# Wider token groups for the seven-product stages of an attention and gated-FFN kernel: three of 1024 tokens and two of 768 in place of six of 768

## The chip, the cores and the metric

The kernel runs on one core of a Trainium2 chip. The metric is the device time of one execution in microseconds. Below, PE is TensorE (PEld its weight loads), DVE is VectorE, ACT is ScalarE, POOL is GpSimd, and SP is SyncE, whose queue issues every DMA of this kernel.

## What is computed

Sliding-window attention over 8 batches of 576 tokens with 8 heads of 64, and behind it a gated feed-forward layer over all 4608 tokens (d_model 512, d_ff 1536), in float32:

```python
scores = scale * np.matmul(q, k.transpose(0, 1, 3, 2))
bias = slopes[:, None, None] * (-np.abs(rel).astype(np.float32))[None, :, :]
mask = (rel >= 0) & (rel < window)            # window = 128
scores = np.where(mask, scores + bias[None], -1000000000.0)
attn = np.exp(scores - np.max(scores, axis=-1, keepdims=True))
attn = attn / (np.sum(attn, axis=-1, keepdims=True) + 1e-09)
x = np.matmul(attn, v)                         # to (4608, 512)
gate = 1.0 / (1.0 + np.exp(-(x @ w_gate)))
val = x @ w_val
out = gate * val @ w_out
```

## The kernel before

Float32 products are made on PE from split operands: each factor becomes a high part and a low part (a cast, then a subtraction, in `parts`), and a product takes three matmuls: high by high, low by high, high by low.

The work has three stages.

1. **Attention** (up to about 305 us), in units of one batch and one pair of heads. PE makes scores (line 408), transposes (456) and values (493); DVE, ACT and POOL do the softmax. x goes to device memory (`xs`). In between, PE makes the **early stage** (`ffn`, matmuls on line 545): the first four of twelve 128-wide chunks of d_ff, for the first 3072 tokens, in blocks of 512 tokens, with plain products.
2. **The seven-product stage** (`ffn2`, line 679). Gate and value projections of one chunk are taken as a 2x2 product of blocks: two halves of d_model, two halves of a token group, in seven products instead of eight. x of a group is read (`later_xr`, one buffer, tag `xr`), combined and split into seven pairs `xc0` to `xc6` (tags `ar0` to `ar6`), each with one buffer. A chunk then runs the products in the order 0, 3, 4, 1, 5, 2, 6, six matmuls each, with DVE adding, ACT copying and taking tanh between them; the hidden rows (`later_hs`, two buffers, four in the last group) are stored to `hid`. Half a group is N2 = 384 tokens, so a matmul has 384 columns.
3. **The down stage** (`last`, line 797), also in seven products. Hidden rows of a group are read into twelve tiles (`rows`), combined and split into pairs `duo` (a ring of eight over tags `ar0` to `ar7`), and multiplied by prepared blocks of w_out (`wo`), 252 matmuls a group. Six groups follow each other.

Prepared weights of a chunk (`prepare2`: seven blocks, high and low, 14 KB a partition) lie in eight resident slots `w2s0` to `w2s7`; three are filled during attention, five behind it in memory that attention used. Chunks 4 to 7 and 0 to 3 are the first eight; groups 4 and 5 use all of them, since the early stage doesn't reach their tokens; then chunks 8 to 11 replace 0 to 3 in slots 4 to 7, and groups 5, 4, 0, 1, 2, 3 use those (0 to 3 with chunks 4 to 7 as well). In the same time w_out is prepared and kept in device memory (`stash_o`), and its six pairs (`wo`) are read into slots 0 to 5 at the end of the last group, each when PE has left the slot.

Nothing is scheduled by hand. Each operation is put into a graph with its engine, a cost and the keys that it reads and writes; `Graph.order` simulates the engines with these costs and always starts what can start first, and the program is written out in that order. So each engine, and SP's queue of DMAs, has a fixed order, and an instruction that waits holds up all behind it on its engine. A DMA also waits for the one eight places ahead in the queue (the eight `DMAHW` counters).

The resident slots and the end of the sequence, which the change rewrites, are these lines:

```python
NT2 = NT // (2 * N2)                  # six groups
first = list(zip(range(FC2), stay + First.fcs))
after = list(zip(range(FC2 - FC1, FC2), swap))
both = first[:FC2 - FC1]
```

Of the kernel before, what the change touches and what calls it, by code (L numbers as in the profile page):

```python
# [8 lines left out]
F32 = mybir.dt.float32  # L9
# [31 lines left out]
OUT0, OSTEP = 490.0, 38.0  # L41
# [11 lines left out]
NRAW = 2  # L53

# [109 lines left out]
def attention_gated_ffn(ctx: ExitStack, tc: tile.TileContext, qd, kd, vd, wg, wv, wo, out):  # L164
# [71 lines left out]
    for p in range(1, NPAIR):  # L236
# [24 lines left out]
    PIECE = 3  # L261
# [178 lines left out]
    def probabilities(u, i0):  # L440
# [4 lines left out]
        both = lambda: T(att, f"both{m % NBOTH}", [P, TRI, P], F32)  # L445
# [28 lines left out]
    def values(u):  # L474
# [46 lines left out]
    def ffn(t, w):  # L521
# [29 lines left out]
        for i0 in range(0, n, GRP):  # L551
# [6 lines left out]
            for i in grp:  # L558
# [18 lines left out]
    def combo(k, part_):  # L577
        return T(moe, f"xc{k}", [P, 4 * N2], F32R, tag=f"ar{k}").rearrange("p (h c t) -> p h c t", h=2, c=2)[:, part_]
# [47 lines left out]
    def ffn2(t, w, todo, F, ends=False):  # L626
        made = t in held
        held[:] = [t]
        t0 = t * 2 * N2
        xr = lambda: xrow()  # L630
        x = lambda h, k: (lambda: xr()[:, 2 * k:2 * k + 2, h * N2:(h + 1) * N2])
        xk = {(h, k): [("xr", k, (h, e)) for e in range(2)] for h in range(2) for k in range(2)}
        low = lambda: T(moe, "low", [P, 4, N2], F32, tag="h2")
# [33 lines left out]
        def chunk(i, fc):  # L667
# [7 lines left out]
            def product(k, b, start, wk):  # L675
                def six():
                    for c in range(2):
                        for j, (xp, wp) in enumerate(((0, 0), (0, 1), (1, 0))):
                            nc.tensor.matmul(mm[b][:, 0:N2], w.tile2(i, wp)[:, wk, c * P:(c + 1) * P], combo(k, xp)[:, c],  # L679
# [36 lines left out]
            move(lambda: hid[c, q, t][m].rearrange("p (h t) -> p h t", h=2), lambda: hs(e), [kp, kv], [("hid", fc, t, 0)], F, N2, True)  # L716
# [248 lines left out]
```

## Time and profile before

| | |
|---|---|
| time, median of 3 runs | 1009.13 us (1007.08 to 1009.23) |
| the profiled execution | 1008.67 us, of which the span from first to last instruction is 1007.0 us |
| granted TensorE clock, mean | 0.995 |
| matmuls | 576 early, 2352 seven-product, 1512 down |
| moved by DMA | 176.89 MB, mean 176 GB/s |
| the early stage's last matmul starts | 330.8 us |
| the down stage's first matmul starts | 740.3 us |

A row of the groups gives line, engine, operation, what it writes and reads, shape and count, then the busy time, the mean duration of one in ns, and the engine's idle time just before them with what ended it. A row of a timeline gives start, duration, engine and operation. A row of the chain of work that ended last gives start, duration and what ran.

### The profile page before, as it was taken

Reading aid. Unit: us, or ns where it says so; the run is one execution under the profiler, and the core shown is the slowest. Engines: PE = TensorE matmul, PEld = TensorE weight load, DVE = VectorE, ACT = ScalarE, POOL = GpSimd, SP = SyncE. Lnnn points to the kernel's source line nnn. Section 1 sums busy time; section 2 is a strip of 40 time slices with the busy share of each in tenths; the row PEclk is TensorE's granted clock in tenths of the full one; section 3 lists DMA queues with packets and bytes.
Section 4 is the critical chain, followed back from the end, with each engine's and each line's share of the span. In section 5 each row is a group of like instructions: output and inputs, shape, how many; then the busy total and the mean of one; then the engine's idle time right before and its main releaser. Section 6 shows DMA issues by size and latency. Waiting matters only on the chain.

```text
span 1007.0 us, 19232 instructions
## 1 busy us (share of the span) xinstructions
PE 985.4 (98%) x6790; PEld 920.5 (91%) x6790; DVE 781.0 (78%) x2039; ACT 540.4 (54%) x1428; POOL 121.9 (12%) x217
## 2 busy tenths in 40 slices
PE   8799899999999999999999999999999999999998
PEld 7577678787888999999999999999999999999998
DVE  7998889877758988945876858758489887869773
ACT  5999788877764545534543536335344443434341
POOL 1334444323330100000000000000000000000000
PEclk9899999999999999999999999999999999999999
DMA  7677777857524543311463443437785454453501
GB/s 271 218 268 242 260 235 243 284 179 240 177 99 159 188 142 128 108 63 48 162 230 136 162 159 130 162 150 268 301 322 195 113 187 125 150 153 101 183 19 63
DMA packets 84288, 176.89 MB, mean 176 GB/s; under 512 B 7648, under 2 KB 50016, under 8 KB 84192
## 3 DMA queue, kind: packets, MB, share of 16 engines
q1 hardware_dynamic: 84192, 175.67, 51.3%
q8 instruction: 53, 0.87, 0.4%
q14 instruction: 43, 0.35, 0.1%
HBM read 117.44 MB, written 58.20 MB: 174 GB/s over the span
## 4 chain that ended last, share of the span: by engine, by line
PE 89%; ACT 5%; DVE 5%; issue 1%; POOL 0%; ACTq 0%; POOLq 0%
PE mm L679 40%; PE mm L797 26%; PE mm L545 10%; PE mm L493 5%; PE mm L408 4%; PE mm L456 3%; ACT pb L431 2%; ACT both L185 1%; ACT pb L451 1%; PE mm L255 1%; DVE xc L194 0%; DVE early_hs L564 0%; DVE w2s L194 0%; DVE mm L420 0%; DVE first L194 0%
## 5 line engine op out<-in xcount | busy, mean ns | idle before, releaser
L679 PE MATMUL mm<-xc,w2s 128*128 128x384 f32 x2352 | 409.4, 334 | 1.2 <-ACT low L185 1.1
L679 PEld LDWEIGHTS mm<-xc,w2s 128*128 128x128 f32 x2352 | 407.4, 188 | 3.0 <-ACT low L185 2.2
L797 PE MATMUL mm<-duo,wo 128*128 128x384 f32 x1512 | 262.4, 334 | 0.0
L797 PEld LDWEIGHTS mm<-duo,wo 128*128 128x128 f32 x1512 | 262.1, 188 | 0.0
L545 PE MATMUL mm<-first,first 128*128 128x512 f32 x564 | 154.1, 409 | 1.6 <-DVE first L194 1.5
L467 POOL TENSOR_SCALAR_AFFINE_SELECT pt<-both 128x384 f32<-128x384 f32 x192 | 103.8, 564 | 188.5 <-ACT both L185 165.1
L545 PEld LDWEIGHTS mm<-first,first 128*128 128x128 f32 x564 | 101.0, 191 | 25.6 <-issue 4.7
L686 DVE TENSOR_TENSOR mm<-mm,low 128x384 f32<-128x384 f32 x112 | 63.0, 562 | 76.9 <-PE mm L679 73.3
L690 ACT ACTIVATE sg<-mm 128x384 f32<-128x384 f32 x112 | 54.8, 491 | 116.7 <-PE mm L679 68.3
L185 ACT COPY low<-mm 128x384 f32<-128x384 f32 x111 | 53.2, 479 | 77.5 <-PE mm L679 68.4
L431 ACT ACTIVATE pb<-pb,st 128x128 f32<-128x128 f32 x216 | 84.8, 401 | 7.2 <-DVE st L428 7.0
L493 PEld LDWEIGHTS mm<-pt,vr 128*64 128x64 f32 x832 | 61.4, 137 | 11.7 <-issue 8.2
L194 DVE TENSOR_TENSOR duo<-rows,duo 128x768 fp32r<-128x768 f32 x66 | 62.9, 956 | 9.8 <-ACT duo L185 7.9
L493 PE MATMUL mm<-pt,vr 128*64 128x256 f32 (+2 forms) x832 | 66.9, 306 | 0.0
L185 ACT COPY both<-mm 128x384 f32<-128x384 f32 x95 | 45.4, 478 | 33.7 <-PE mm L456 21.3
L185 ACT CAST duo<-rows 128x768 fp32r<-128x768 f32 x44 | 36.7, 835 | 48.7 <-PE mm L797 26.0
L420 DVE COPY_PREDICATED mm<-early_h,mm 128x256 f32<-128x256 int32 (+1 forms) x144 | 48.5, 392 | 10.5 <-PE mm L408 10.2
L428 DVE CUSTOM_DVE_ANT_0 pb<-mm,early_h 128x128 f32<-128x128 f32 x216 | 51.3, 282 | 0.0
L456 PE MATMUL mm<-ident,pb 128*128 128x128 f32 x216 | 38.3, 286 | 10.9 <-ACT both L185 8.9
L456 PEld LDWEIGHTS mm<-ident,pb 128*128 128x128 f32 x216 | 25.5, 142 | 22.7 <-ACT both L185 12.7
L408 PE MATMUL mm<-kr,qr 64*64 64x192 f32 (+1 forms) x792 | 44.8, 337 | 1.4 <-DVE mm L249 1.1
L431 ACT ACTIVATION_READ_ACCUMULATOR pb<-pb,st 128x1 f32 x216 | 42.7, 198 | 0.0
(122 smaller groups left out, 1104.9 us busy)
## 6 DMA issues: line engine op xcount, KB each, us to landing
hid<-later_hs SPq DMA_DIRECT2D x56, 384.0 KB, 2.3
rows<-hid SPq DMA_DIRECT2D x48, 384.0 KB, 3.9
kr<-in_k_dram SPq DMA_DIRECT2D x21, 576.0 KB, 5.6
wo<-stash_o SPq DMA_DIRECT2D x12, 896.0 KB, 8.1
vr<-in_v_dram SPq DMA_DIRECT2D x32, 288.0 KB, 3.1
xs<-xt SPq DMA_DIRECT2D x32, 288.0 KB, 3.0
stash_o<-wtmp SPq DMA_DIRECT2D x12, 768.0 KB, 3.4
rows_xr<-hid SPq DMA_DIRECT2D x24, 384.0 KB, 3.5
```

The costliest lines, as they stand in the source:

```text
L185: g.add("ACT", act_cost(n, psum), lambda: nc.scalar.copy(out(), src()), reads, writes, want, release=release, ways=[("DVE", dve_cost(n, ps ...
L194: g.add("DVE", dve_cost(n, psum, True), lambda: nc.vector.tensor_tensor(out(), a(), b(), op=ALU.subtract), reads, writes, want, port=not p ...
L408: nc.tensor.matmul(to, qraw(u)[rows, i // 2, h * D:(h + 1) * D], keys, start=True, stop=True)
L431: g.add("ACT", 0.39, lambda: nc.scalar.activation(pb()[:, e], pb()[:, e], AF.Exp, bias=st()[:, e:e + 1], scale=-1.0, accum_out=st()[:, 3 + ...
L456: nc.tensor.transpose(tp[:, e], pb()[:, e], ident)
L467: nc.gpsimd.affine_select(pt(u)[:, f0:f0 + 2 * n - 1:2, :], both(), [[0, n], step], cmp, 0.0, base=0, channel_multiplier=mult)
L493: nc.tensor.matmul(to()[e * D:(e + 1) * D, a - e * S - t0:b - e * S - t0], vraw(u)[:, c], seen, start=first, stop=last, skip_group_check=True)
L545: nc.tensor.matmul(mm[s][:, 0:wd], w.tile(kind, wi, i)[:, c * P:(c + 1) * P], xpart(x, c)[:, 0:wd], start=(k == 0 and c == 0), stop=(k == ...
L679: nc.tensor.matmul(mm[b][:, 0:N2], w.tile2(i, wp)[:, wk, c * P:(c + 1) * P], combo(k, xp)[:, c], start=(start and c == 0 and j == 0), stop ...
L686: g.add("DVE", dve_cost(N2, psum=True), lambda: nc.vector.tensor_tensor(o(), bk(b)(), a(), op=ALU.add), [("mm", b), *reads] if okeys else ...
L690: g.add("ACT", act_cost(N2, psum=True), lambda: nc.scalar.activation(sg[h](), bk(b)(), AF.Tanh, scale=0.5), [("mm", b)], [("sg", h)], F)
L797: nc.tensor.matmul(mm[b][:, 0:N2], wo2(2 * q + m, wp)[:, k, j * P:(j + 1) * P], duo(xp)[:, m], start=(k in (0, 3, 1) and q == 0 and m == 0 ...
```

## The change

The token groups become three of 1024 tokens (halves of 512 columns) and two of 768 (halves of 384). Tiles of the stages are sized for 512. To find room:

- seven weight slots stay resident instead of eight. Slots 0 to 2 hold chunks 4 to 6 as before, slots 3 to 6 first chunks 0 to 3 and then chunks 7 to 10. Chunks 4 and 11 share slot 0: both are written to device memory once (`stash`, two DMAs of 896 KB each), and each of the groups 0 to 2 begins with the one that lies in slot 0, fetches the other (`fetch`) and uses it after slots 1 and 2;
- the early stage's split operands take six tiles of four pieces instead of eight of three, so tag `ar6` is free during attention and holds the first of three buffers of k and q; the buffers `both` and one of `xt` move into parts of `xr` and `h2`;
- in the down stage the ring of `duo` has six places instead of eight, and the twelve row tiles lie in `xr` (4), slot 6 (3), `hs0`, `hs1`, `ar6` (2) and `h3` instead of `xr` (4) and slots 6 and 7 (8).

Groups 3 and 4 (768 tokens) come first with seven chunks each, then 4 and 3 with the other five, then groups 0, 1 and 2 with eight.

The diff, cut to its core:

```diff
-SPLIT = 4
+GROUPS = ((0, 512), (1024, 512), (2048, 512), (3072, 384), (3840, 384))
+NG = len(GROUPS)
+SPLIT = 3
...
-N2 = 384
...
+NSLOT2 = 7
...
-OUT0, OSTEP = 490.0, 38.0
+OUT0, OSTEP = 470.0, 36.0
...
+ROOM = {"h2": 4 * NB, "h3": 6 * 2 * P, "h4": 4 * NB, "xr": 2 * KC * NB, "ar6": 4 * NB}
...
-    PIECE = 3
+    PIECE = 4
...
-    slots = {"kr": keep("h2", TOK), "qr": keep("xr", (NBLK + 1) // 2, P)}
+    slots = {("kr", 2): keep("h2", TOK), ("qr", 2): keep("xr", (NBLK + 1) // 2, P),
+             ("kr", 0): keep("ar6", TOK), ("qr", 0): keep("ar6", (NBLK + 1) // 2, P)}
     kept = [keep("h2", TRI, P), keep("xr", TRI, P)]
+    spread2 = [keep("xr", TRI, P), keep("h2", TRI, P)]
+    xt0 = keep("xr", S)
...
-        both = lambda: T(att, f"both{m % NBOTH}", [P, TRI, P], F32)
+        both = lambda: spread2[m % NBOTH]
...
-        t0 = t * 2 * N2
+        t0, N2 = GROUPS[t]
...
-    RING = (7, 0, 3, 4, 1, 5, 2, 6)
+    def stash(i, fc):
+        for p in range(2):
+            move(lambda p=p: stash2[KEPT.index(fc)][p], lambda p=p: as32(w2.tile2(i, p).rearrange("p a f -> p (a f)")),
+                 [("w2", i, p, 0), ("w2", i, p, 2)], [("stash2", fc, p)], FIRST + 0.95, 896, True)
+
+    def fetch(i, fc):
+        for p in range(2):
+            move(lambda p=p: as32(w2.tile2(i, p).rearrange("p a f -> p (a f)")), lambda p=p: stash2[KEPT.index(fc)][p],
+                 [("stash2", fc, p)], [("w2", i, p, 0), ("w2", i, p, 2)], FIRST + 0.95, 896, True)
+
+    RING = (0, 3, 4, 1, 5, 2)
...
+    HOMES = ((4, "xr", "xr", KC), (7, "w2s6", "w2s6", 3), (8, "hs0", "hs0", 1), (9, "hs1", "hs1", 1), (11, "ar6", "ar6", 2), (12, "h3", "h3", 1))
...
-    first = list(zip(range(FC2), stay + First.fcs))
-    after = list(zip(range(FC2 - FC1, FC2), swap))
-    both = first[:FC2 - FC1]
-    for i, fc in first[:KEEP2]:
-        prepare2(w2, i, fc, 2.0e6 + i, P0 + PSTEP * i)
+    KEPT = (stay[0], swap[3])
+    for i in range(KEEP2):
+        prepare2(w2, i, stay[i], 2.0e6 + i, P0 + PSTEP * i)
+    stash(0, stay[0])
...
-    ffn2(late[-1], w2, first[FC2 - FC1:] + both, FIRST + 1)
-    for i, fc in after:
+    head = list(zip(range(KEEP2), stay))
+    body = list(zip(range(KEEP2, NSLOT2), first))
+    ffn2(SPLIT, w2, head + body, FIRST + 0.4)
+    ffn2(SPLIT + 1, w2, body + head, FIRST + 1)
+    body = list(zip(range(KEEP2, NSLOT2), stay[KEEP2:] + swap))
+    for i, fc in body + [(0, swap[3])]:
         prepare2(w2, i, fc, FIRST + 0.9)
+    stash(0, swap[3])
...
+    for t in (SPLIT + 1, SPLIT):
+        ffn2(t, w2, body + [(0, swap[3])], FIRST + 1)
+    here, gone = swap[3], stay[0]
     for t in range(SPLIT):
...
-        ffn2(t, w2, both + after if t < SPLIT - 1 else both + [after[z] for z in (2, 0, 1, 3)], FIRST + 1, t == SPLIT - 1)
+        ffn2(t, w2, [(0, here)], FIRST + 1, ends)
+        fetch(0, gone)
+        here, gone = gone, here
+        ffn2(t, w2, head[1:] + [(0, here)] + body, FIRST + 1, ends)
```

Since a planner writes the order, three places of it are shown. Names end in a tile number of the program; in brackets stands what a row waits for.

SP's queue in group 0, where the next group's x is asked for. Before:

```order
L190 DMA later_xr_3972<-xs2_100 128x4x384 [waits DMAHW3_49,DVE_49]
L190 DMA stash_o0_106<-wtmp1_5642 128x1536 [waits DMAHW4_49,DVE_49]
L190 DMA later_xr_3972<-xs1_99 128x4x384 [waits DMAHW5_49,DVE_49]
L190 DMA hid010_118<-later_hs0_4140 128x768 [waits DMAHW6_49,DVE_49]
L190 DMA hid110_136<-later_hs1_4202 128x768 [waits DMAHW7_49,DVE_49]
L190 DMA wraw0_206<-in_moe_w_out_dram 128x1024 [waits DMAHW0_49]
```

After (`w2s00` and `w2s01` are the two parts of slot 0, `stash20` is chunk 4 in device memory):

```order
L192 DMA later_xr_3961<-xs2_100 128x4x192 [waits DMAHW2_49,DVE_49]
L192 DMA later_xr_3961<-xs3_101 128x4x320 [waits DMAHW3_49]
L192 DMA later_xr_3961<-xs1_99 128x4x128 [waits DMAHW4_49,DVE_49]
L192 DMA later_xr_3961<-xs2_100 128x4x384 [waits DMAHW5_49]
L192 DMA stash_o1_107<-wg0_5352 128x256 [waits DMAHW6_49,Activation_49]
L192 DMA w2s00_1395<-stash20_142 128x1792 [waits DMAHW7_49,PE_49]
L192 DMA w2s01_1404<-stash20_142 128x1792 [waits DMAHW0_49]
L192 DMA stash_o1_107<-wg0_5352 128x256 [waits DMAHW1_49,Pool_49]
L192 DMA hid120_137<-later_hs0_4119 128x1024 [waits DMAHW2_49,DVE_49]
```

The two reads of slot 0 are new; they stand behind the x of the next group and a store that waits for ACT, and ahead of the stores of hidden rows.

SP's queue at the border to the down stage (`rows` are the row tiles of its first group, `rows_xr` at the end those of the next). Before:

```order
L190 DMA wo250_7461<-stash_o5_111 128x1792 [waits DMAHW2_49,PE_49]
L190 DMA wo251_7465<-stash_o5_111 128x1792 [waits DMAHW3_49]
L190 DMA hid123_145<-later_hs2_7264 128x768 [waits DMAHW4_49,DVE_49]
L190 DMA rows70_7541<-hid100_130 128x2x384 [waits DMAHW5_49,PE_49]
L190 DMA rows71_7543<-hid110_136 128x2x384 [waits DMAHW6_49]
L190 DMA rows_xr_7073<-hid001_113 128x2x384 [waits DMAHW7_49,DVE_49]
```

After:

```order
L192 DMA wo250_7005<-stash_o5_111 128x1792 [waits DMAHW2_49,PE_49]
L192 DMA wo251_7008<-stash_o5_111 128x1792 [waits DMAHW3_49]
L192 DMA hid122_139<-later_hs2_6751 128x1024 [waits DVE_49]
L192 DMA rows_ar6_7074<-hid020_122 128x2x512 [waits DMAHW5_49,PE_49]
L192 DMA rows_h3_7076<-hid110_132 128x2x512 [waits DMAHW6_49,DMAHW4_49]
L192 DMA rows_ar6_7074<-hid120_137 128x2x512 [waits DMAHW7_49]
L192 DMA rows_xr_6633<-hid001_113 128x2x512 [waits DVE_49]
```

Before, tiles in slot 7 stand behind the wait for PE's last product, and its tiles in slot 6 have been read earlier; now the two tiles in `ar6` wait for that product, and the one in `h3` stands between them.

DVE at the seam from attention to the seven-product stage, up to the split of `xc0` and `xc1`. Before:

```order
L194 TENSOR_TENSOR xc5_4070<-later_xr_3972,xc5_4070 128x768 [waits PE_49]
L308 TENSOR_SCALAR tt_1420<-tt_1420 128x512 [waits Activation_49]
L311 SCALAR_TENSOR_TENSOR wbits0_442<-wraw0_206,wbits0_442 128x512 [waits DMAHW5_49]
L564 SCALAR_TENSOR_TENSOR early_hs0_1028<-sg0_878,mm0_148 128x512 [waits DMAHW7_49,PE_49]
L311 SCALAR_TENSOR_TENSOR tt_1420<-wraw1_224,tt_1420 128x512 [waits DMAHW6_49,DVE_49]
L194 TENSOR_TENSOR xc6_4102<-later_xr_3972,xc6_4102 128x768 [waits Activation_49]
L311 SCALAR_TENSOR_TENSOR tt_1420<-wraw1_224,tt_1420 128x512 [waits DVE_49]
L564 SCALAR_TENSOR_TENSOR early_hs1_1205<-sg1_947,mm1_149 128x512 [waits DMAHW0_49,PE_49]
L194 TENSOR_TENSOR xc0_4117<-later_xr_3972,xc0_4117 128x768 [waits Activation_49]
L194 TENSOR_TENSOR xc1_4127<-later_xr_3972,xc1_4127 128x768 [waits Activation_49]
```

After:

```order
L196 TENSOR_TENSOR xc4_4080<-low_4034,xc4_4080 128x2x384 [waits Activation_49]
L313 TENSOR_SCALAR tt_1410<-tt_1410 128x512 [waits Activation_49]
L316 SCALAR_TENSOR_TENSOR wbits0_434<-wraw0_201,wbits0_434 128x512 [waits DMAHW1_49]
L572 SCALAR_TENSOR_TENSOR early_hs1_1195<-sg1_937,mm1_145 128x512 [waits DMAHW2_49,PE_49]
L316 SCALAR_TENSOR_TENSOR tt_1410<-wraw1_219,tt_1410 128x512 [waits DMAHW0_49,DVE_49]
L196 TENSOR_TENSOR xc0_4103<-later_xr_3961,xc0_4103 128x2x384 [waits Activation_49]
L196 TENSOR_TENSOR xc1_4106<-later_xr_3961,xc1_4106 128x2x384 [waits Activation_49]
L196 TENSOR_TENSOR xc5_4117<-later_xr_3961,xc5_4117 128x2x384 [waits Activation_49]
```

The split of `xc5` moves behind those of `xc0` and `xc1`; the weight work between them stays. On PE, 117 matmuls of the early stage stand behind the last attention values before, and 99 after.

More of the change, by code (lines that the diff above doesn't have):

```diff
@@ L240, in attention_gated_ffn @@
     stash_o = [dram.tile([2, P, 7 * 2 * P], F32, name=f"stash_o{i}") for i in range(NFC // 2)]
-    hid = {(c, q, t): dram.tile([2, P, 2 * N2], F32, name=f"hid{c}{q}{t}")
-           for c in range(2) for q in range(NDUO) for t in range(NT2)}
+    hid = {(c, q, t): dram.tile([2, P, 2 * n2], F32, name=f"hid{c}{q}{t}")
+           for c in range(2) for q in range(NDUO) for t, (_, n2) in enumerate(GROUPS)}
+    stash2 = [dram.tile([2, P, 7 * 2 * P], F32, name=f"stash2{i}") for i in range(2)]
     mm = [ps_m.tile([P, NB], F32, name=f"mm{i}") for i in range(8)]
@@ L281, in tile2 @@
         def tile2(self, i, part_):
+            if i == NSLOT2 - 1:
+                return T(pools["w2"], f"w2s{i}", [P, 2, 7, 2 * P], F32R)[:, part_]
             return T(moe if i < KEEP2 else pools["w2"], f"w2s{i}{part_}", [P, 7, 2 * P], F32R)
@@ L568, in ffn @@
                 while a < end:
-                    n2 = a // (2 * N2)
-                    b = min((n2 + 1) * 2 * N2, end)
-                    move(lambda c=c, q=q, m=m, n2=n2, a=a, b=b: hid[c, q, n2][m, :, a - n2 * 2 * N2:b - n2 * 2 * N2],
+                    n2 = a // (2 * NB)
+                    b = min((n2 + 1) * 2 * NB, end)
+                    move(lambda c=c, q=q, m=m, n2=n2, a=a, b=b: hid[c, q, n2][m, :, a - n2 * 2 * NB:b - n2 * 2 * NB],
                          lambda h=h, a=a, b=b: h()[:, a - t * NB:b - t * NB], [("hs", e, 0), ("hs", e, 1)],
@@ L860, in attention_gated_ffn @@
     w2 = Later()
[L861 to L866 removed]
+    first, stay, swap = First.fcs, list(range(FC1, NFC - FC1)), list(range(NFC - FC1, NFC))
+    KEPT = (stay[0], swap[3])
+    for i in range(KEEP2):
+        prepare2(w2, i, stay[i], 2.0e6 + i, P0 + PSTEP * i)
+    stash(0, stay[0])
     def follow(keys):
         g.add("PY", 0.0, lambda: None, [], keys, FIRST)
[L871 removed]
+    for a in range(6):
         follow(piece_keys(a) + [("ar", a, j) for j in range(2)])
[L873 removed]
+    follow(["w2pool", "s2", "a1", "u2", ("wtmp", 0), ("wtmp", 1), ("ar", 6, 0), ("ar", 6, 1)])
     later_xr = [("xr", k, (h, e)) for k in range(2) for h in range(2) for e in range(2)]
     follow([("xr", c, e) for c in range(KC) for e in range(2)] + ["w2pool"] + later_xr)
[L876 to L877 removed]
+    for i in range(FC1):
+        prepare2(w2, KEEP2 + i, first[i], FIRST + 0.5)
     if banks[0] == 2:
@@ L880, in attention_gated_ffn @@
         g.add("PY", 0.0, lambda: None, [], [TP, TAIL], FIRST)
-    late = list(range(SPLIT, NT2))
-    for t in late[:-1]:
-        ffn2(t, w2, first, FIRST + (0.4 if t == SPLIT else 1))
-    ffn2(late[-1], w2, first[FC2 - FC1:] + both, FIRST + 1)
-    for i, fc in after:
+    head = list(zip(range(KEEP2), stay))
[4 more added lines that the diff above has]
+    for i, fc in body + [(0, swap[3])]:
         prepare2(w2, i, fc, FIRST + 0.9)
+    stash(0, swap[3])
     follow([("wbits", 1), ("wg0", 0), ("wg0", 1)])
```

96 lines of the change are left out of this document (45 added, 51 removed).

## The prediction

> **What bounds the kernel now.** I read the page first, then the busy times by stage, PE's waits, the chain that ended last, and last the timelines of the places the change touches. The page's first rows:
>
> ```profile
> span 1007.0 us, 19232 instructions
> PE 985.4 (98%) x6790; PEld 920.5 (91%) x6790; DVE 781.0 (78%) x2039; ACT 540.4 (54%) x1428; POOL 121.9 (12%) x217
> ```
>
> The same by stage (columns: stretch, its length, then PE, PEld, DVE, ACT, POOL busy, granted clock, DMA share, GB/s):
>
> ```profile
> 0.00:100.00 100.00, 87.48 (x922) 69.03 (x923) 87.01 (x448) 84.17 (x329) 31.91 (x65) 0.97 0.74 250
> 100.00:200.00 100.00, 95.55 (x909) 75.53 (x908) 88.20 (x393) 80.20 (x295) 45.32 (x73) 0.98 0.77 255
> 200.00:300.00 100.00, 100.00 (x946) 80.97 (x945) 72.37 (x394) 74.57 (x284) 33.57 (x68) 1.00 0.56 179
> 300.00:340.00 40.00, 39.51 (x200) 33.51 (x199) 33.11 (x50) 19.10 (x30) 4.47 (x6) 1.00 0.47 158
> 340.00:700.00 360.00, 360.00 (x2077) 359.64 (x2076) 273.85 (x467) 166.60 (x318) 6.67 (x8) 1.00 0.41 144
> 700.00:720.00 20.00, 19.30 (x110) 18.66 (x109) 6.70 (x13) 6.05 (x14) 0.00 (x0) 1.00 0.73 281
> 720.00:1004.00 284.00, 283.58 (x1636) 283.20 (x1635) 219.80 (x279) 109.59 (x161) 0.00 (x0) 1.00 0.47 156
> ```
>
> PE loses 12.5 us in the first 100 us and 4.5 in the next 100; from 200 us on it loses about 1.2 us until it ends. PE's own list of waits agrees: behind the attention copies, and hardly at all in the seven-product stages (columns: us in total, times, longest).
>
> ```profile
> PE mm L456 <- ACT both L185: 8.9, 12, 1.8
> PE mm L679 <- ACT low L185: 1.1, 2, 0.6
> ```
>
> So two thirds of the kernel, from 331 us on, is one queue of matmuls. What counts there is their number times the spacing from one start to the next. Not the mean duration: matmuls overlap, and the mean contains the pipeline's tail.
>
> ```profile
> L679 PE MATMUL mm<-xc,w2s 128*128 128x384 f32 x2352 | 409.4, 334 | 1.2 <-ACT low L185 1.1
> L797 PE MATMUL mm<-duo,wo 128*128 128x384 f32 x1512 | 262.4, 334 | 0.0
> ```
>
> The spacing at 384 columns is read from the chain's last piece, all down-stage matmuls (start, us, what):
>
> ```profile
> 742.54 261.06 PE mm L797 x1506
> ```
>
> Take off one duration: (261.06 - 0.33) / 1505 = 173.2 ns. At 512 columns the dense tail of the early stage tells it, in PE's timeline, with one duration (min/median/max, ns) from the view of line 545:
>
> ```profile
> 312.69 18.52 PE L545 MATMUL mm<-first,first 128*128 128x512 f32 x81
> 331.06 6.70 PE L679 MATMUL mm<-xc,w2s 128*128 128x384 f32 x36
> ```
>
> ```profile
> L545 PE MATMUL mm<-first,first x564: 387/393/793, 50.9 to 330.8; 128*128 128x512 f32 x188
> ```
>
> (18.52 - 0.39) / 80 = 226.6 ns. 128 columns more cost 53.4 ns, 0.417 each; so 384 columns account for 160.2 ns and **13.0 ns is paid per matmul**, however wide.
>
> **The change, part by part.** The sum goes against the profiled execution, 1008.67 us for a span of 1007.0; the median of the three runs is 1009.13, 0.46 above it.
>
> *Fewer, wider matmuls.* Before: 2352 + 1512 = 3864 at 384 columns. After: a chunk pass is 42 matmuls, a group's down stage 252. Three groups of 1024 make 24 passes and three down stages, 1008 + 756 = 1764 at 512 columns; two groups of 768 make 24 passes and two down stages, 1512 at 384. The columns are the same, 588 matmuls are gone. 3864 x 0.1732 = 669.2 us becomes 1764 x 0.2266 + 1512 x 0.1732 = 399.7 + 261.9 = 661.6: **-7.6 us**, all on the path, since PE is what ends last. If the 512 spacing is off by 0.5 ns, this moves by 0.9.
>
> The trace speaks against the size a page of the skill would give. The Trainium skill's "TensorE: Matmul & The Clock Gate", section "Wait — 56ns, not 53.3ns?", puts the fixed cost of a back-to-back matmul at about 2.5 ns. By that, 588 matmuls would be worth 1.5 us. The rows above hold 13.0 for this pairing of weight loads and matmuls, so the measurement decides.
>
> *DVE and ACT.* Their work per column stays, with fewer instructions, and x is split seven ways six times instead of seven. In 340 to 700 us DVE is busy 273.85 of 360, so this is hidden: 0. Per product the ratio holds too: PE's six matmuls go from 1.04 to 1.36 us (x1.31), a DVE pass by the next rows from 956 ns at 768 elements to some 1220 at 1024, between 956 and 1485 (x1.28).
>
> ```profile
> L194 DVE TENSOR_TENSOR duo<-rows,duo 128x768 fp32r<-128x768 f32 x66 | 62.9, 956 | 9.8 <-ACT duo L185 7.9
> L194 DVE TENSOR_TENSOR w2s<-tt,w2s 128x1280 fp32r<-128x1280 f32 x11 | 16.3, 1485 | 0.1
> ```
>
> *The seam from attention to the seven-product stage.* The last attention values on PE, and DVE's timeline, which has no gap from the first weight cast on:
>
> ```profile
> 302.39 2.08 PE L493 MATMUL mm<-pt,vr 128*64 128x256 f32 x26
> ```
>
> ```profile
> 304.56 0.22 DVE L186 COPY xt<-mm 128x64 f32<-128x64 f32 x1 [7.63 <-PE mm L493]
> ...
> 311.31 0.42 DVE L186 CAST w2s<-wbits 128x512 fp32r<-128x512 f32 x1
> 332.41 2.07 DVE L194 TENSOR_TENSOR xc<-later_xr,xc 128x768 fp32r<-128x768 f32 x2
> ```
>
> From the first weight cast (it needs attention's memory) to xc0 are 332.41 + 1.0 - 311.31 = 22.1 us of DVE work, just in time for PE. In the order of before 117 early-stage matmuls stand on PE behind the last attention values (L493), in that of the change 99: attention ends 18 x 0.2266 = 4.1 us later against the same end of PE's early work, and DVE's 22 us (I take 21.6 for the change, whose order has a cast of 1280 and a small pass more there, an xc and an integer pass fewer) start from there. After the last L493 the cast waits for the copy and the store of xt (3.0 us):
>
> ```profile
> xs<-xt SPq DMA_DIRECT2D x32, 288.0 KB, 3.0
> ```
>
> About 4.5 + 21.6 = 26.1 us. PE comes for the low half of xc0 after 99 x 0.2266 + 14 x 0.173 = 24.9. A wait of 1.2 us, against 0.5 now: **+0.7**. Bounds: -0.5 (no wait) and +3.5 (DVE starting 311.31 - 304.47 = 6.8 us after the last L493, as it does now).
>
> *Slot 0 exchanged through memory, three times.* PE reads the reloaded slot ten products after it left it, 10 x 1.36 = 13.6 us. In SP's queue stand ahead of the reload up to four loads of x (2.1 MB) and a store that waits for ACT or POOL; behind it stand the stores of hidden rows, which have a second buffer. The rates that x and the weights have now, and the time to landing of a 896 KB weight (min/median/max):
>
> ```profile
> 570.00:579.00 9.00, 9.00 (x53) 9.00 (x53) 8.90 (x18) 3.62 (x8) 1.63 (x3) 1.00 0.78 250
> 700.00:710.00 10.00, 10.00 (x59) 9.76 (x57) 2.01 (x4) 1.70 (x4) 0.00 (x0) 1.00 0.97 399
> DMA to landing us min/median/max: 4.4/8.1/10.3
> ```
>
> x at 250 GB/s takes 8.4 us and is asked for some 2.5 us before the slot is free (the last split of x stands two products ahead of the slot's last one), the 1.8 MB of weights at 399 take 4.6, and I allow 2 for the ends: 8.4 + 4.6 + 2 - 2.5 = 12.5 us after release, 1 us before PE. Not hidden by much. I take **+0.5** for all three; bounds 0 and +11 (10.3 us to landing behind 7 us of x, 3.7 late each time).
>
> *The last group before the down stage.* Now PE waits 0.6 us and slips by as much again near 710 us, where stores that free a hidden-row buffer land late behind the wo loads:
>
> ```profile
> stash_o<-wtmp SPq DMA_DIRECT2D x2, 768.0 KB, 10.7
> ```
>
> After, the chunks are 9.5 us apart instead of 7.3 and wo's loads with them; but a reload comes in front of those stores. **-0.7**; bounds -1.3 and +3.
>
> *The border to the down stage.* Three of twelve row tiles now lie in ar6 and h3 and are fetched only when PE has left its last product; before, only the two in slot 7 were. From there: 5 to 7 us to land three tiles of 512 KB (384 KB took 3.9), then five DVE passes of about 1.2; the second tile pair is wanted 48 matmuls later, 48 x 0.2266 = 10.9, and the third at 13.6. That leaves about 1 us: **+0.3**; bounds 0 and +4. The ring of split rows shrinks from eight to six; the first group apart, PE's order takes the products there as before, and L797 waits 0.0 now: 0.
>
> ```profile
> rows<-hid SPq DMA_DIRECT2D x48, 384.0 KB, 3.9
> ```
>
> *Attention.* Slot 0 is also stored once (1.8 MB) at about 110 us, where the DMA engines are full and PE already loses 2.4 of 10 us:
>
> ```profile
> 110.00:120.00 10.00, 7.62 (x78) 5.78 (x77) 9.96 (x56) 7.27 (x32) 5.13 (x6) 0.97 0.92 337
> ```
>
> The two stores stand in SP's queue ahead of loads of q, v and k; the second waits for a POOL pass. At 337 GB/s they push those loads back 5.4 us, and loads run two units ahead. From there on PE's order differs a little up to 300 us. **+0.5**; bounds -2 and +3. The tiles moved from attention's pool to shared ones cost nothing: no instruction is added.
>
> Sum: 1008.67 - 7.6 + 0.7 + 0.5 - 0.7 + 0.3 + 0.5 = 1002.4; towards the median a little more, and the bounds of the unknown terms lean up. I say **1002.5**.
>
> **The rivals.**
>
> *The 13 ns is not per matmul in these stages.* If the spacing grows with the columns alone, 512 cost 173.2 x 4/3 = 230.9 ns, the 7.6 us vanish, and the other terms leave 1010.0: no change. For it: the early stage reads other tiles. Against: same shapes of weights, same type, 81 in a row at 226.6. Chance 0.05. By the 2.5 ns of the Trainium skill's "TensorE: Matmul & The Clock Gate", section "Wait — 56ns, not 53.3ns?", it would be 1.5 us less; the trace does not agree with it.
>
> *Slot 0 comes too late.* The first product of the reloaded slot waits, in each of three groups. Price: what the landing exceeds 13.6 us by, three times. With the rest at -6.8 the kernel turns slower by over 0.2% from 9.3 us on, that is from 16.7 us after release; at the bound, 17.3, it ends at 1013. For it: x and weights share one set of DMA engines, and the store ahead of the reload can hold SP. Against: 12.5 worked out above. Chance 0.05.
>
> *Attention and the seam take half back.* Loads pushed back by the stores cost 3 us, and DVE starts as late after attention as now, 3.5: 1008.67 - 7.6 + 6.5 + 0.1 = 1007.7, within 0.2%. For it: PE waits most in this part. Against: DVE has 7.6 us idle before the seam. Chance 0.09; a partial one, 1005 to 1007, 0.12.
>
> That the change does not do what it says is excluded by the order: the products stand there with 512 columns for groups 0 to 2.
>
> **How the numbers follow.** The forecast, 998.5 to 1005, has 0.67; better than that (the seam free, attention shorter) 0.02. The partial rival is faster too: faster 0.81. Within 0.2% (2 us, about what a measurement of this kernel can tell from no change), 1007.1 to 1011.1: 0.05 + 0.09 = 0.14. Slower 0.05. The range 998.5 to 1007 takes forecast and partial rival, 0.79, with the bounds of seam and attention one at a time.
>
> **What would show it.** Right: L679 and L797 in two shapes, spaced 226.6 and 173.2 ns, some 661.6 us together; PE's wait on xc at about 331 us near 1 us; no wait on w2s at the second use of slot 0. Wrong: a 512-column spacing near 231; PE waits behind w2s00<-stash20 of microseconds; PE losing more than 18 us before 200 us.

## The result and the profile after

The change runs in **1000.55 us** (median, 1000.26 to 1000.78) against 1008.67 us for the kernel before (1007.08 to 1009.23): ratio **0.992**, 95% interval 0.990 to 0.994. Predicted were 1002.5 us, range 998.5 to 1007. A fourth run of the change, slowed to 1623.34 us at a granted clock of 0.557, counts in its median but neither in its range nor in the ratio; the median of the other three is 1000.32. Two later measurements of the same kernel gave 998.92 and 1000.19 us, ratios 0.9899 (0.9883 to 0.9914) and 0.9923 (0.9908 to 0.9938).

The profiled execution took 1000.32 us, 8.35 less than that of before, for a span of 998.6. PE's groups of the two big stages (columns as before: what, count, busy us, mean ns, idle before):

```profile
L687 PE MATMUL mm<-xc,w2s 128*128 128x512 f32 x1008 | 228.9, 389 | 0.0
L687 PE MATMUL mm<-xc,w2s 128*128 128x384 f32 x1008 | 175.4, 334 | 0.1
L817 PE MATMUL mm<-duo,wo 128*128 128x512 f32 x756 | 171.9, 389 | 0.2 <-DVE duo L196 0.2
L817 PE MATMUL mm<-duo,wo 128*128 128x384 f32 x504 | 87.6, 334 | 0.0
```

The counts are those of the prediction: 1764 matmuls at 512 columns and 1512 at 384. Start to start, with waits left out, they take 226.76 and 173.38 ns in the trace; at 384 columns it was 173.36 before.

By stage (stretch, length, then PE, PEld, DVE, ACT, POOL busy, granted clock, DMA share, GB/s):

```profile
0.00:100.00 100.00, 87.55 (x922) 69.12 (x923) 86.95 (x448) 84.03 (x329) 31.86 (x65) 0.97 0.74 250
100.00:200.00 100.00, 94.98 (x879) 75.00 (x878) 83.36 (x380) 79.96 (x293) 43.44 (x70) 0.98 0.77 265
300.00:340.00 40.00, 39.87 (x217) 34.20 (x214) 31.71 (x50) 18.94 (x32) 2.81 (x6) 1.00 0.42 142
340.00:700.00 360.00, 360.00 (x1816) 326.53 (x1815) 269.99 (x424) 162.60 (x280) 12.71 (x12) 1.00 0.50 180
700.00:760.00 60.00, 59.80 (x263) 48.91 (x262) 40.40 (x45) 25.45 (x36) 0.00 (x0) 1.00 0.73 250
```

PE is as full as before. Up to 200 us it loses 17.5 us (before: 17.0), from 300 to 760 us 0.33. The stash and the reloads show as traffic, 180 GB/s in place of 144 from 340 to 700 us, and in no wait of PE. The weight loads are no longer busy all the time: 326.53 of 360 us, where they had 359.64.

The chain's long pieces (start, us, what) give the balance:

```profile
334.36 391.81 PE mm L687 x1960
727.88 8.42 DMA hid<-later_hs
736.33 6.13 DMA rows_h<-hid
747.37 247.76 PE mm L817 x1210
```

PE ends at 747.37 + 247.76 = 995.13 us; before at 742.54 + 261.06 = 1003.60. The seven-product stage's first matmul starts at 331.61 us, before at 331.06. So the two product stages went from 672.54 to 663.52 us, **-9.02**, and all ahead of them from 331.06 to 331.61, +0.55. Of the 9.02, matmuls make 3864 x 173.36 = 669.86 against 1764 x 226.76 + 1512 x 173.38 = 662.15 us, **-7.71**. The other 1.31 are waits: 2.68 us of PE's time before was not matmul spacing, 1.37 after.

Where they lie, as the parts over the normal spacing of gaps that exceed it by 0.1 us or more, each with the 0.11 us that is lost once more at the next start: before 1.04 us at the seam (333.7 and 338.3 us), 1.35 in the last group (695.5, 710.7, 714.2); after 0.41 at the seam (334.4), 0.11 in the last group (734.5) and 0.47 at the border to the down stage (747.4). The border's part is not steady: in the profiles of the two later measurements of the change it is 0 and 0.39.

### The profile page after: what moved, and what is told of

It reads as the page before. It is cut to its first block, busy times and chain, and to the rows that moved or that the text cites. A ratio compares the mean times of both kernels' runs of the same rounds, so it can differ in the third digit from the quotient of the medians.

```text
span 998.6 us, 17735 instructions
## 1 busy us (share of the span) xinstructions
PE 977.3 (98%) x6202; PEld 843.6 (84%) x6202; DVE 771.5 (77%) x1951; ACT 525.1 (53%) x1350; POOL 124.5 (12%) x217
## 4 chain that ended last, share of the span: by engine, by line
PE 87%; ACT 5%; DVE 5%; DMA 2%; issue 1%; POOL 0%; ACTq 0%; POOLq 0%; DVEq 0%
PE mm L687 39%; PE mm L817 25%; PE mm L553 10%; PE mm L501 5%; PE mm L416 4%; PE mm L464 3%; ACT pb L439 2%; DMA hid<-later_hs 1%; ACT pb L459 1%; PE mm L258 1%; DMA rows_h<-hid 1%; DVE mm L428 1%; ACT early_xr L187 1%; DVE wbits L316 0%; DMA kr<-in_k_dram 0%
## 5 line engine op out<-in xcount | busy, mean ns | idle before, releaser
L687 PE MATMUL mm<-xc,w2s 128*128 128x384 f32 (+1 forms) x2016 | 404.1, 362 | 0.1
L687 PEld LDWEIGHTS mm<-xc,w2s 128*128 128x128 f32 x2016 | 363.8, 188 | 40.3 <-DVE xc L196 0.5
L817 PE MATMUL mm<-duo,wo 128*128 128x512 f32 (+1 forms) x1260 | 259.2, 367 | 0.2 <-DVE duo L196 0.2
L817 PEld LDWEIGHTS mm<-duo,wo 128*128 128x128 f32 x1260 | 229.2, 188 | 30.2 <-DVE duo L196 0.6
L694 DVE TENSOR_TENSOR mm<-mm,low 128x384 f32<-128x384 f32 (+1 forms) x96 | 60.3, 629 | 72.3 <-PE mm L687 72.1
L698 ACT ACTIVATE sg<-mm 128x384 f32<-128x384 f32 (+1 forms) x96 | 52.0, 544 | 117.9 <-PE mm L687 71.9
L187 ACT COPY low<-mm 128x512 f32<-128x512 f32 (+1 forms) x93 | 49.6, 534 | 71.3 <-PE mm L687 65.1
L475 POOL TENSOR_SCALAR_AFFINE_SELECT pt<-early_h 128x384 f32<-128x384 f32 x96 | 53.1, 576 | 93.1 <-ACT early_h L187 90.7
L475 POOL TENSOR_SCALAR_AFFINE_SELECT pt<-early_xr 128x384 f32<-128x384 f32 x96 | 50.2, 546 | 100.7 <-ACT early_xr L187 91.3
L187 ACT COPY early_xr<-mm 128x384 f32<-128x384 f32 (+2 forms) x72 | 31.5, 460 | 21.1 <-PE mm L464 13.0
L702 DVE SCALAR_TENSOR_TENSOR later_hs<-sg,later_hs 128x384 f32<-128x384 f32 (+1 forms) x48 | 29.8, 621 | 12.5 <-ACT sg L698 12.5
```

The lines of the kernel that those rows point to most:

```text
L187: g.add("ACT", act_cost(n, psum), lambda: nc.scalar.copy(out(), src()), reads, writes, want, release=release, ways=[("DVE", dve_cost(n, ps ...
L475: nc.gpsimd.affine_select(pt(u)[:, f0:f0 + 2 * n - 1:2, :], both(), [[0, n], step], cmp, 0.0, base=0, channel_multiplier=mult)
L694: g.add("DVE", dve_cost(N2, psum=True), lambda: nc.vector.tensor_tensor(o(), bk(b)(), a(), op=ALU.add), [("mm", b), *reads] if okeys else ...
L698: g.add("ACT", act_cost(N2, psum=True), lambda: nc.scalar.activation(sg[h](), bk(b)(), AF.Tanh, scale=0.5), [("mm", b)], [("sg", h)], F)
L817: nc.tensor.matmul(mm[b][:, 0:N2], wo2(2 * q + m, wp)[:, k, j * P:(j + 1) * P], duo(xp)[:, m], start=(k in (0, 3, 1) and q == 0 and m == 0 ...
```

## The experiments

A kernel's own spread over its runs is 1 to 5 us, and part of it arises in attention: in three profiles of the change itself the seven-product stage starts at 331.61, 331.07 and 330.69 us. So terms under 1 us are read in the trace, in the product stages, and the times bound them.

### The width alone

Control, the change without an edit:

> The change itself, on the chip and beside the runs of before that the next three share. Expected 1000.5 us, ratio 0.992; the other kernels of this call are compared with it.

Measured: 998.92 us (998.40 to 999.39), before 1009.09; ratio 0.9899 (0.9883 to 0.9914).

Then the change's structure with the widths of before:

```diff
-GROUPS = ((0, 512), (1024, 512), (2048, 512), (3072, 384), (3840, 384))
+GROUPS = tuple((768 * t, 384) for t in range(6))
-SPLIT = 3
+SPLIT = 4
```

(The early stage's stores to `hid` are cut at 768 tokens again.)

> Everything of the change except the widths: seven slots, stash and reload of slot 0, the moved tiles and the shorter ring stay, but the tokens are six groups of 768 again, all with 384 columns (and the exchange of slot 0 runs four times). Theory (13 ns are paid per matmul, whatever its width): the 588 matmuls come back, 3864 x 173.3 against 1764 x 226.7 + 1512 x 173.3 ns, +7.7 us on the change: 1008.2 us, the same as before within 0.2%. Reloads stay hidden: PE has 10 to 13 products of 1.04 us between slot 0's two chunks, 10.4 us or more, and the reloads of the change landed within 9.6 us of their issue. Rival (the gain came from the new structure: fewer stalls, another order of the weights' preparation): the time stays within 1.5 us of the change, 1000 to 1002. If the truth lies between, the share of the 7.7 us that comes back tells how much is the width's.

Measured: 1008.99 us, ratio to before **0.9997** (0.9989 to 1.0006). PE's groups of this kernel:

```profile
L687 PE MATMUL mm<-xc,w2s 128*128 128x384 f32 x2352 | 408.8, 334 | 0.1
L817 PE MATMUL mm<-duo,wo 128*128 128x384 f32 x1512 | 262.5, 334 | 1.4 <-DVE duo L196 1.4
```

With the old widths the whole gain is gone; the structure by itself brings nothing in sum (its gaps at the seam and in the last group are smaller than before, and a new one stands at the border). It lies 10.1 us above the control, more than the 7.7 expected. Its profile is 8.8 above the control's: the matmuls 7.8, waits in the product stages 2.0 more, and 1.0 less ahead of them. Most of the 2.0 stands at the border (1.4 on `duo` above); the chain of this kernel there:

```profile
732.73 9.47 DMA hid<-later_hs
742.22 5.01 DMA rows_h<-hid
748.13 0.96 DVE duo L196
```

The store of a hidden row takes 9.5 us, its reader waits for it, and DVE for that. It is the same chain as in the change, where store and read take 8.42 and 6.13 us and PE is idle for 0.2.

### Where the 13 ns come from

A kernel of matmuls alone, 120 to a stream, at several widths n and in two types t:

```python
nc.tensor.matmul(mm[b][:, 0:n], w[t][:, wp, k, c * P:(c + 1) * P], x[t][:, xp, c, 0:n],
                 start=(c == 0 and j == 0), stop=(c == 1 and j == 2), skip_group_check=True)
```

> Matmuls alone: leaves out everything of the reference except PE; 120 matmuls a stream (six into one bank, a weight load each, the kernel's float32 split type) at 512, 448, 384, 320, 256, 192 and 128 columns, then bf16 at 512, 384, 256 and 128. Nothing else runs beside them. Theory: the spacing from start to start is 13.3 ns + 0.417 ns a column: 226.6, 199.9, 173.2, 146.6, 119.9, 93.2 and 66.6 ns. Rival 1 (the 13 ns come from the rest of the kernel, from other engines at work or from waits between products): 512 at 213 to 216 and 384 at 160 to 163. Rival 2 (a weight load sets a floor for narrow matmuls): the line bends at some width and the narrow ones all take the same. What bf16 does is open; if the 13 ns hang on the type it lies below the line.

Groups of its streams (`xr` is the kernel's split type, fp32r in DVE's rows, `xb` bf16):

```profile
L48 PE MATMUL mm<-xb,wb 128*128 128x512 bf16 x117 | 25.7, 379 | 0.2
L48 PE MATMUL mm<-xr,wr 128*128 128x384 f32 x120 | 21.0, 334 | 0.0
L48 PE MATMUL mm<-xr,wr 128*128 128x256 f32 x120 | 14.6, 283 | 0.0
L48 PE MATMUL mm<-xr,wr 128*128 128x128 f32 x120 | 13.5, 274 | 0.0
L48 PE MATMUL mm<-xb,wb 128*128 128x128 bf16 x120 | 6.9, 219 | 0.0
```

Busy less one duration, over one less than the count, is the spacing: at 384 columns (21.0 - 0.334) / 119 = 173.7 ns. Start to start, in the trace (ns):

| columns | 512 | 448 | 384 | 320 | 256 | 192 | 128 |
|---|---|---|---|---|---|---|---|
| split type | 226.7 | 202.7 | 173.3 | 146.7 | 120.0 | 111.7 | 111.7 |
| bf16 | 216.0 | | 162.5 | | 109.2 | | 55.8 |

The cost is there with nothing beside PE (rival 1 falls): 13.3 ns and 0.417 a column from 256 to 512, but for 448, which is 3 above the line. Below 256 the line bends to a floor of 111.7 (rival 2 holds there, outside the widths of the product stages). And it hangs on the type: bf16 pays 2.6.

Do weight loads make it? The second half of another kernel without the rest (its first half follows below) loads 128, 64 or 32 weight columns, and so makes as many output rows. Rows of its groups:

```profile
L67 PE MATMUL mm<-xr,wr 128*32 128x512 f32 x60 | 14.1, 394 | 0.0
L67 PE MATMUL mm<-xr,wr 128*128 128x512 f32 x60 | 13.8, 389 | 0.0
L67 PE MATMUL mm<-xr,wr 128*128 128x256 f32 x60 | 7.4, 283 | 0.0
L67 PE MATMUL mm<-xr,wr 128*64 128x256 f32 x60 | 7.0, 276 | 0.0
L67 PE MATMUL mm<-xr,wr 128*128 128x128 f32 x60 | 6.8, 274 | 0.0
L67 PE MATMUL mm<-xr,wr 128*64 128x128 f32 x60 | 3.8, 222 | 0.0
```

At 128 columns the floor of 111.7 ns falls to 60.0 with half the weight columns. At 256 columns the spacing falls from 120.0 to 113.3, so there half of the 13.3 ns goes with them; a quarter of the weight columns gives the same as half. At 512 columns it doesn't fall: 64 and 32 weight columns give 229.9 and 231.7, no less than 226.7. So the number of weight columns is a part of the cost at 256 columns and doesn't explain it at 512. What in this type makes the cost stays open. Weight columns and output rows were changed together, so these streams don't tell the two apart.

### The same number, other widths

```diff
-GROUPS = ((0, 512), (1024, 512), (2048, 512), (3072, 384), (3840, 384))
+GROUPS = ((0, 512), (1024, 512), (2048, 512), (3072, 512), (4096, 256))
```

> The last 1536 tokens are cut 1024 + 512 and not 768 + 768: the number of matmuls (3276) and of columns stays that of the change, 756 of them go from 384 to 512 columns and 756 from 384 to 256. Theory (a fixed cost per matmul and 0.417 ns a column): the same time as the change, 1000.5 within 1 us. Rival (at 256 columns something else sets the pace, a weight load or DVE's passes over half as many columns, 0.72 us a product): each of the 756 narrow matmuls takes longer than 119.9 ns; at 136 ns, the mean busy time of a weight load in the change, it is +12 us, 1012.7.

Measured: 1002.95 us (1001.64 to 1006.09), ratio 0.9945 (0.9931 to 0.9960). Its groups at 256 columns:

```profile
L687 PE MATMUL mm<-xc,w2s 128*128 128x256 f32 x504 | 61.9, 284 | 0.9 <-DVE later_hs L702 0.5 <-DVE later_hs L694 0.2 <-ACT low L187 0.2
L817 PE MATMUL mm<-duo,wo 128*128 128x256 f32 x252 | 30.4, 283 | 0.0
```

Spacing 119.8 and 120.0 ns: no floor yet at 256, so count and columns do set the pace, and the 12 us of the rival don't come. But the time is 2 to 4 us above the three times of the change: PE waits for DVE's and ACT's work on products, 0.9 us at 256 columns and 1.5 at 512, nearly all while the two newly cut groups run, and slips by nearly as much again (gaps between starts sum to 4.5 us). The theory held for the spacing and missed these waits.

### The exchange of slot 0

The reload used at once, and the reload left out:

```diff
-        ffn2(t, w2, head[1:] + [(0, here)] + body, FIRST + 1, ends)
+        ffn2(t, w2, [(0, here)] + head[1:] + body, FIRST + 1, ends)
```

> In groups 0 to 2 the reloaded chunk of slot 0 is the first one behind the fetch and no longer the third, so the planner can put only 3, 4 and 5 products of 1.36 us (4.1, 5.4, 6.8 us) on PE between slot 0's last use and its next, where the change has 10 (13.6). Theory (the reload lands about 9.5 us after PE left the slot, and its place behind the chunks of slots 1 and 2 is what hides it): PE waits 5.4 + 4.1 + 2.7 = some 12 us on w2s in the three groups, 1009 to 1013 us. Rival (the reload is short, 5 us as a lone transfer of 1.8 MB would be): waits of 1 us or less, 1000 to 1002 us. My prediction had put the landing at 12.5 us after the release; by that the waits are 21 us and the time 1021.

```diff
-        fetch(0, gone)
```

> The change without its six reloads of slot 0; leaves out the exchange, so groups 0 to 2 multiply one chunk with the weights of another, and 5.5 MB less are read. Theory (reload hidden, its traffic disturbs nothing): within 1 us of the change. Rival (it costs, by its traffic and its place in SP's queue ahead of the stores of hidden rows): 0.5 us faster or more for my price, up to 3 us for late hidden-row buffers; it would show as PE waits that vanish between 500 and 700 us.

Without the exchange: 998.85 us, ratio 0.9903 (0.9888 to 0.9918), beside the control's 998.92 and 0.9899. **The exchange is free** where the change has it; no term of 0.5 us is left. The trace agrees: from the first seven-product matmul to the last of the down stage it is 663.45 us without the exchange, 662.87 in the control.

Used at once: 1017.62 us, ratio 1.0084 (1.0068 to 1.0099). PE's list of waits, and its timeline at the first reload (idle before in brackets):

```profile
PE mm L687 <- DMA w2s<-stash: 8.8, 6, 2.0
```

```profile
523.90 0.51 PE L687 MATMUL mm<-xc,w2s 128*128 128x512 f32 x1 [1.39 <-DMA w2s<-stash]
526.38 18.91 PE L687 MATMUL mm<-xc,w2s 128*128 128x512 f32 x75 [1.98 <-DMA w2s<-stash]
```

The reload was issued at 518.46 us, when PE left the slot: the parts are there 5.4 and 7.9 us later. In the change PE leaves the slot at 519.4 and comes back at 532.84, after 13.4 us, so some 5.5 are to spare, not the 1 that I had worked out. The third reload has less: its second part lands 9.6 us after its own issue, 10 after the first part's, and some 3 are left. The SP queue of the change shows why, at the first reload (start, issue time):

```profile
514.20 2.64 SPq L192 DMA_DIRECT2D later_xr<-xs  x4
519.43 0.81 SPq L192 DMA_DIRECT2D w2s<-stash  x2
```

x is asked for 5.2 us ahead of the reload, not 2.5, and what is behind it moves at some 400 GB/s.

The waits alone don't explain the time: 8.8 us are listed, and its profile is 15.7 us above the control's. Gaps between starts sum to 10.1; the rest is in the granted clock (columns as in the view by stage):

```profile
523.00:527.00 4.00, 1.13 (x3) 0.71 (x4) 3.16 (x3) 0.00 (x0) 0.00 (x0) 0.94 1.02 403
527.00:530.00 3.00, 3.00 (x9) 2.33 (x8) 0.00 (x0) 1.07 (x2) 0.00 (x0) 0.51 1.03 430
530.00:534.00 4.00, 4.00 (x19) 3.28 (x18) 0.39 (x1) 1.17 (x2) 0.00 (x0) 1.00 0.84 337
```

Behind each of the three pairs of waits about eight matmuls run at 427 ns, 200 more than normal: 3 x 8 x 0.2 = 4.8 us. The theory of this run was right that the place in the order hides the reload, and had waits of 12 us for these 10; it did not have the clock. The 21 us by my own landing time are refuted.

### What a wait costs

Matmuls alone: stretches of 48 or 54 at 512 columns, and between them a wait for 1 to 6 passes of DVE, which write the next moving operand.

```python
nc.vector.tensor_copy(d[:, 0, 0:P], mm[(turn[0] - 1) % 8][:, 0:P])
for p in range(passes - 1):
    nc.vector.tensor_copy(d[:, (p + 1) % 2, 0:896], d[:, p % 2, 0:896])
nc.vector.tensor_copy(x["r"][:, 0, 0, 0:P], d[:, (passes - 1) % 2, 0:P])
```

> Matmuls alone again; leaves out everything of the reference except PE. 512 columns in the kernel's split type, in 18 stretches of 48 or 54 with a wait for 1 to 6 DVE passes between them (waits of about 0.6 to 5 us), then streams of 60 with weights of 128, 64 and 32 columns at 512, 256 and 128 columns. First question, what a wait costs beyond itself: with the reload used at once two waits of about 2 us, ten matmuls apart, were followed by eight matmuls at 427 ns instead of 227. Theory: a wait over about 2 us, or two close ones, makes the granted clock fall to about half for 3.4 us, so it costs 1.6 us more than its length; shorter ones cost their length alone. Rival: the clock fell there because the DMA engines were full at the same time, and here nothing follows a wait. Second question, where the 13 ns of this type come from: if from loading 128 weight columns, 64 and 32 columns bring the spacing at 512 columns towards 216 ns, what bf16 had; rival: it stays at 226.7, and the 13 ns hang on the moving operand.

PE's timeline, seven of the stretches (start, us, and in brackets the wait ahead):

```profile
50.78 12.55 PE L48 MATMUL mm<-xr,wr 128*128 128x512 f32 x54 [0.64 <-DVE xr L59]
64.64 11.17 PE L48 MATMUL mm<-xr,wr 128*128 128x512 f32 x48 [1.31 <-DVE xr L59]
77.78 12.53 PE L48 MATMUL mm<-xr,wr 128*128 128x512 f32 x54 [1.97 <-DVE xr L59]
92.94 12.77 PE L48 MATMUL mm<-xr,wr 128*128 128x512 f32 x48 [2.63 <-DVE xr L59]
...
167.54 14.17 PE L48 MATMUL mm<-xr,wr 128*128 128x512 f32 x54 [1.97 <-DVE xr L59]
...
200.42 15.14 PE L48 MATMUL mm<-xr,wr 128*128 128x512 f32 x54 [3.29 <-DVE xr L59]
...
292.75 12.58 PE L48 MATMUL mm<-xr,wr 128*128 128x512 f32 x54 [3.29 <-DVE xr L59]
```

48 matmuls take 11.17 us, or 12.77 when slowed; 54 take 12.55 or 14.17. No wait of 0.64 or 1.31 us slowed anything (three of each); of those of 1.97 us and more, ten in twelve did, by 1.6 us or, twice, by 2.6 to 2.9. Hardly any DMA ran beside, so full DMA engines are not needed for it.

Which waits slowed it hangs on their moment, and the trace shows how. The clock changes only at borders that lie 3.41 us apart, or a multiple of that. These are the stretches between borders around two of the waits (columns: stretch, length, then PE, PEld, DVE, POOL busy, granted clock, DMA share, GB/s):

```profile
165.08:168.50 3.42, 1.45 (x7) 0.90 (x6) 1.77 (x4) 0.00 (x0) 1.00 0.00 0
168.50:171.91 3.41, 3.41 (x10) 2.63 (x9) 0.00 (x0) 0.00 (x0) 0.50 0.02 5
287.96:291.38 3.42, 1.50 (x7) 0.92 (x5) 1.78 (x4) 0.00 (x0) 1.00 0.00 0
291.38:294.79 3.41, 2.04 (x9) 1.67 (x10) 1.25 (x3) 0.00 (x0) 1.00 0.00 0
```

The wait of 1.97 us ahead of 167.54 lay in one stretch, PE was busy for 1.45 us of it, and the next stretch ran at half clock. The wait of 3.29 us ahead of 292.75 was divided by a border, PE was busy for 1.50 and 2.04 us, and the clock stayed. In this run every stretch at full clock with 1.93 us or more of idle PE was followed by one at half clock, and none with 1.91 us or less. A stretch at half clock was followed by another where 0.84 or 1.20 us of it were idle: those are the two larger costs. With the reload used at once, the stretches ahead of the three slow ones had 2.78, 1.91 and 2.47 us of idle PE, so the limit is near 1.9 us. This was read from the traces; no run was made to test it.

### Attention's store, and when w_out is prepared

The stash of slot 0 moved out of attention, behind the preparation of the later chunks:

```diff
-    stash(0, stay[0])
...
     for i, fc in body + [(0, swap[3])]:
         prepare2(w2, i, fc, FIRST + 0.9)
```

> The two stores of chunk 4 of slot 0 (1.8 MB) are taken out of attention: they come with the preparation of the later chunks. Theory (they push loads of q, k and v back where the DMA engines are full): attention ends 0.5 us earlier and with it all, 1000.0; bound 3 us. Rival (they are hidden): the same as the change within 0.5 us, with PE's busy time before 300 us as in the change.

Measured: 1000.33 us, ratio 0.9916 (0.9902 to 0.9929). PE's busy time from 100 to 200 us is 94.97 us with the store elsewhere, 94.98 with it there. The stores cost nothing that these runs can tell; what PE loses there against before (95.55) has another source, not found here.

The two numbers that set when w_out is prepared, put back in the change and put in before:

```diff
-OUT0, OSTEP = 470.0, 36.0
+OUT0, OSTEP = 490.0, 38.0
```

> The change with the preparation of w_out at its old times (from 490 us in steps of 38, not from 470 in steps of 36). Theory: the earlier preparation is what moved the late stores of w_out away from the last group, where before lost 0.7 and 0.3 us near 710 and 714 us; with the old times some of that comes back, up to +1.2 us. Rival: it makes no difference, within 0.4 us, and the vanished waits come from the longer chunks.

> The kernel before with one edit of the change alone: w_out is prepared from 470 us in steps of 36 instead of from 490 in steps of 38. Theory (those two numbers, which my prediction gave no term of their own, removed the late stores near 710 us; the change lost about 1 us when they were set back): before without its waits of 0.7 and 0.3 us near 710 us, 1 us faster, 1007.8. Rival (in the shorter chunks of before the preparation is late whenever it is asked for, so only the longer chunks cured it): the same as before within 0.3 us, with the waits near 710 us still there.

> The change once more, beside the same runs of before. Expected 998.5 to 1001 us, as it measured 1000.55 and 998.92 so far.

Measured: the change with the old numbers 1001.43 us, ratio 0.9929 (0.9915 to 0.9943); before with the new ones 1008.71, ratio 1.0004 (0.9994 to 1.0013); the change again 1000.19, ratio 0.9923 (0.9908 to 0.9938). PE's timeline in the change with the old numbers (idle before in brackets):

```profile
696.77 38.77 PE L687 MATMUL mm<-xc,w2s 128*128 128x512 f32 x168 [0.68 <-ACT low L187]
735.99 1.65 PE L687 MATMUL mm<-xc,w2s 128*128 128x512 f32 x6 [0.45 <-DVE later_hs L694]
```

As gaps between starts PE is late there by 0.84, 0.21 and 0.61 us in the last group (696.8, 701.2 and 736.0 us), which the change is not. So in the trace of the change the new numbers are worth 1.9 us in the last group, less the 0.47 that it loses at the border; the times, 0.9929 against 0.9899 to 0.9923, neither confirm nor exclude that much. In before they remove the gaps near 710 us too, but one of 0.33 appears at 491, and the time is the same within 0.1%. That they explain the vanished waits is likely, and that they shorten before by themselves is excluded beyond 0.6 us.

## Why the prediction was right

- **Fewer, wider matmuls: -7.6 predicted, -7.7 measured**, and with the widths put back the time of before came back (ratio 0.9997). The rival that the 13 ns are not per matmul falls: 120.0, 173.3 and 226.7 ns with nothing else running. The Trainium skill's "TensorE: Matmul & The Clock Gate", section "Wait — 56ns, not 53.3ns?", gives 2.5 ns, and 215.7 and 55.6 ns at 512 and 128 columns. For bf16 these runs agree (216.0 and 55.8); for this kernel's type they show 13.3.
- **The seam, +0.7 predicted, -0.6 measured.** The step that failed first is DVE's start, put 4.5 us after the last attention values. These rows of the change (PE, then DVE) show 2.7:

```profile
307.02 2.08 PE L501 MATMUL mm<-pt,vr 128*64 128x256 f32 x26
309.03 22.74 PE L553 MATMUL mm<-first,first 128*128 128x512 f32 x99
```

```profile
311.80 0.43 DVE L188 CAST w2s<-wbits 128x512 fp32r<-128x512 f32 x1 [0.47 <-DMA xs<-xt]
333.35 2.69 DVE L196 TENSOR_TENSOR xc<-later_xr,xc 128x768 fp32r<-128x768 f32 x3
```

  From 309.10 to the cast at 311.80, then 22.5 us of work to xc0 at 334.30 (21.6 predicted; DVE stands idle twice in it, for 1.25 us): 25.2 us, where PE came at 24.9. The wait is 0.3 and not 1.2. The other step is the 0.5 of before that I set against it. It is no wait for xc0, which cost 0.15; it stands behind an ACT copy, seven microseconds into the stage:

```profile
338.25 7.03 PE L679 MATMUL mm<-xc,w2s 128*128 128x384 f32 x39 [0.49 <-ACT low L185]
```

  With its slip it cost 0.77, and in the change it is gone, which I had not foreseen. The upper bound of +3.5 was the whole wait, without those 0.5 taken off.
- **The exchange, +0.5 predicted, 0 measured.** Right that it is hidden, wrong by how little: 12.5 us to landing were 8 in the first group, where x is asked for earlier than I took it to be, and 10 in the third. Its rival needed 16.7.
- **The last group, -0.7 predicted, -1.2 measured.** Its waits went almost altogether; I had left half for the reload in front of the stores. The cause I gave, longer chunks with later loads of `wo`, is not shown: with the old numbers for w_out such waits are back in chunks just as long, and those two numbers, part of the change, had no term in my sum.
- **The border, +0.3 predicted, +0.5 measured (0 and 0.4 in the other two profiles of the change).** Right in place, with another link: the reader of `h3` waits for a store that takes 8.4 us, before DVE's passes begin.
- **Attention, +0.5 predicted, +0.55 measured, for a reason that does not hold.** The stores are free; and 0.55 is within the 0.9 us by which the change differs from itself there, so that the numbers agree is luck. Its rival, 3 us, did not come.

In sum the mechanism and its large term were right, and the small terms, +1.3 together, came out at -0.75: -7.7 - 0.75 = -8.45 against the profile's -8.35. That is why the forecast lay 2 us high.

## What to carry to other kernels

Where PE is one queue of matmuls, count them and read the spacing from start to start at two widths, both wide enough to lie above the floor: the part that does not grow with the columns is paid per matmul, and wider tiles save just that. A resident operand may be exchanged through device memory for nothing if PE has more products between its two uses than the landing takes; ordered too close, the same exchange cost 16 us in the profile and 19 in the medians. Small terms that all lean one way add up: an undisturbed seam can as well get better.

## What the runs showed of the hardware

- A wait of PE of 2 us or more can cost more than its length: in ten of twelve cases the granted clock fell to half for some 3.4 us (eight matmuls at 427 ns), 1.6 us more. In that run it fell behind each stretch of 3.41 us, between fixed borders, in which PE was idle for 1.93 us or more, so a wait that a border divides may cost nothing beyond its length: 1.97 us at 77.78 did not. The Trainium skill's "TensorE: Matmul & The Clock Gate", section "HAM oscillation — how this bites in real kernels", asks for no gap over about 3.4 us; here 1.97 was enough twice in three times, and 1.31 never.
- From 256 to 512 columns the split type pays 13.3 ns for each matmul and bf16 2.6. The split type has a floor of 111.7 ns at 192 and 128 columns; with half the weight columns 128 columns take 60.0 and 256 take 113.3 in place of 120.0.
